# One hand-placed plan for linear attention and a gated unit on one core

## The chip, the core and the metric

The kernel runs on one core of one Trainium2 chip, as one launch. The core has five engines with a queue each: TensorE (PE; its weight loads are shown apart as PEld), VectorE (DVE), ScalarE (ACT), GpSimd (POOL) and SyncE (SP), which only issues transfers here. Each engine takes its instructions in the order in which the program puts them into its queue; semaphores make it wait for the others. Sixteen DMA engines move data between HBM and SBUF. Products land in PSUM, in eight banks.

The metric is the device time of one execution in microseconds (us).

## The reference

Eight batches, eight heads, 576 positions, heads of 64: linear attention without softmax, a norm over each head, and then a gated unit over the 512 columns of all heads.

```python
# q, k, v: (8, 8, 576, 64) float32; w_val, w_out: (512, 512), conv_w: (5, 512), which arrive as float64
kv  = einsum('bhsd,bhse->bhde', k, v)
o   = einsum('bhsd,bhde->bhse', q, kv)
o   = o / sqrt(mean(o*o, -1) + 1e-6) * g_norm
x   = o.transpose(0, 2, 1, 3).reshape(8, 576, 512)
xp  = concat([zeros(8, 4, 512), x], axis=1)
gate_pre = sum(conv_w[t] * xp[:, t:t+576, :] for t in range(5))
gate = 1 / (1 + exp(-gate_pre))
out = (gate * (x @ w_val)) @ w_out
```

## The kernel before

Everything is float32. A batch's positions are taken in 5 chunks of rows (four of 128, one of 64); in a chunk the rows are ordered so that position t*18 + n stands at n*32 + t, which lets the convolution read its five taps as five shifted columns of the same tile (`xT`, with a halo of 4 x 32 columns).

Attention of one batch (`attention(b)`):

- `unit_kv` (line 210), four times, one for each pair of heads: k and v products over 5 pieces of positions into one PSUM tile `kv`; after the fourth VectorE copies it into `kv_bd`, a block-diagonal tile of two heads, and the loads of k and v for batch b + 2 are issued (`load_kv`, line 86; `kl` and `vl` are the last 64 positions, in pieces of 256 bytes).
- `unit_turn_q` (231), four times: VectorE transposes q in blocks of 32 x 32 into `qT`, and the q of batch b + 1 is issued (`load_q`, 103: each row is fetched twice, at two offsets, so that block transposes suffice; 16 transfers of 140 KB for a batch).
- `unit_norm` (238), for each chunk, the short one first: `raw` = q times kv on TensorE (two PSUM banks), squares on ScalarE, sums over a head on VectorE (`ss`), plus epsilon and power -0.5 on GpSimd (`rt`), and the scaled `x` on VectorE.
- `unit_turn_x` (268), two chunks later: TensorE transposes x into PSUM, ScalarE copies it into `xT` with g_norm as scale; after the last chunk but three GpSimd fills the halo.

MLP of one batch (`mlp(b)`):

- `unit_gate` (284), for each of 4 column blocks: ScalarE starts the gate with the last tap, VectorE adds four taps, ScalarE takes the sigmoid.
- `unit_val` (297), for each block: two products of 288 columns (`val`, PSUM tag `mm`, three banks), each multiplied by the gate on VectorE into `gv`.
- `unit_out` (314), 4 or 5 chunks: four products into one bank (tag `mm` as well), a copy on ScalarE into `ot` (three buffers), four stores on SP.

`merge` (353) interleaves the units of attention(b) with those of mlp(b - 1) by their shares of weight, so both lists end together; batch 0's attention is merged with the nine weights (`unit_weights`, 199), which are loaded by GpSimd's queue as 64-bit pairs through three staging buffers and turned into float32 by seven VectorE operations each (`narrow`, 152). The order of the program is not the order in the queues: the framework's scheduler moves instructions by priority and its own estimates of cost.

Most float32 products are two instructions in the trace: the four products of an out chunk are eight rows.

```python
for b in range(B + 1):
    before = mlp(b - 1) if b > 0 else [
        (1.0, lambda n=n: unit_weights(n)) for n in range(len(weights))
    ]
    merge(attention(b) if b < B else [], before)
    if b == 0:
        load_kv(1)
```

Of the kernel before, what the change touches and what calls it, by code (L numbers as in the profile page):

```python
# [9 lines left out]
FP32 = mybir.dt.float32  # L10
# [10 lines left out]
def kernel(  # L21
# [25 lines left out]

    nc = tc.nc
# [15 lines left out]
    S2 = 2 * S  # L64
    assert 2 * T == P and NB * TB == S and SV <= 512 and C <= 512 and D == 2 * TB
# [20 lines left out]
    def load_kv(b):  # L86
        for i in range(2):
            for n, (name, src) in enumerate((("k", k), ("v", v))):
                t = loads.tile([P, H // 2, NJ, D], FP32, tag=f"{name}{i}", name=f"{name}{i}_{b}")
                nc.sync.dma_start(  # L90
                    out=t[:].rearrange("p h j d -> p h (j d)"),
                    in_=src[b, i * H // 2:(i + 1) * H // 2, 0:SF, :].rearrange(
                        "h (p j) d -> p h (j d)", j=NJ),
                )
                st[name, b, i] = t
            if i == 0:
                for n, src in enumerate((k, v)):
# [19 lines left out]
    load_kv(0)  # L117
    for hp in range(HP):
        load_q(0, hp)


    kv_bd = []
    for i in range(2):
        t = const.tile([P, HP, P], FP32, name=f"kvbd{i}")
        nc.vector.memset(t[:], 0.0)
        kv_bd.append(t)
    ident = const.tile([P, P], FP32, name="ident")
    make_identity(nc, ident[:])
    mhalf = const.tile([P, H], FP32, name="mhalf")
    nc.vector.memset(mhalf[:], -0.5)  # L130
    xTs = []
    for i in range(3):
        t = const.tile([P, NK, SX], FP32, name=f"xT{i}")
        for s in range(K - 1):
            nc.gpsimd.memset(t[:, :, s * TB:s * TB + 1], 0.0)
        xTs.append(t)
    gv = const.tile([P, NK, S2], FP32, name="gv")

    gcol = const.tile([P, 1], FP32, name="gcol")
    for r in range(P // D):  # L140
        nc.scalar.dma_start(out=gcol[r * D:(r + 1) * D, :], in_=g_norm.unsqueeze(1))
# [4 lines left out]
    def stage(key, rows):  # L146
        n = rows.shape[0]
        t = loads.tile([P, C, 2], U32, tag="w64", bufs=3, name=f"w64_{key[0]}{key[1]}")
        nc.gpsimd.dma_start(out=t[0:n].rearrange("p c w -> p (c w)"), in_=rows.bitcast(U32))
        staged[key] = t[0:n]  # L150

    def narrow(key, dst):
# [26 lines left out]
        mf = work.tile([P, C], FP32, tag="wmf", name=f"wmf_{key[0]}{key[1]}")[0:n]  # L179
# [4 lines left out]
            out=dst, in0=mf, scalar=2.0 ** -20, in1=e.bitcast(FP32), op0=ALU.mult, op1=ALU.mult,  # L184
        )

    cw = const.tile([K, C], FP32, name="cw")
    wval = const.tile([P, NK, C], FP32, name="wval")
    wout = const.tile([P, NK, C], FP32, name="wout")
    weights = [(("cw", 0), moe_conv_w[:, :], cw[:])]  # L190
    for n, src, dst in (("wval", moe_w_val, wval), ("wout", moe_w_out, wout)):
        for kc in range(NK):
            weights.append(((n, kc), src[kc * P:(kc + 1) * P, :], dst[:, kc, :]))


    nc.vector.tensor_scalar_mul(gcol[:], gcol[:], math.sqrt(D))
    cwT = const.tile([P, NK, K], FP32, name="cwT")

    def unit_weights(n):
        for ahead in range(n + 2 if n else 0, n + 3):  # L200
            if ahead < len(weights):
                stage(*weights[ahead][0:2])
        narrow(weights[n][0], weights[n][2])
        if n == 0:
            cwps = ps("tp", [P, NK, K], "cwps")
            for kc in range(NK):
                nc.tensor.transpose(cwps[:, kc, :], cw[:, kc * P:(kc + 1) * P], ident[0:K, 0:K])
# [196 lines left out]
```

## Time and profile before

| | |
|---|---|
| median of 3 runs | 484.03 us (481.39 to 484.14) |
| the profiled execution | 481.39 us, span 479.6 us |
| mean granted TensorE clock | 0.936 of full speed |
| busy: TensorE, VectorE, ScalarE, GpSimd | 374.6, 235.0, 111.8, 90.0 us |
| moved by DMA | 51.23 MB, mean 107 GB/s |
| the chain that ended last | PE 56%, DVE 17%, POOL 7%, DMA 7%, issue 6%, ACT 4% |

The profile is one execution. The span is the time from the first instruction to the last; the 1.8 us between it and the run's time lie around it. Matmuls are pipelined, so the length of one matmul is longer than the distance to the next one; the price of a product is read from starts. Idle time of an engine that isn't the bottleneck costs nothing.

### The profile page before, as it was taken

The numbers are of one execution on the slowest core, as the hardware profiler recorded it, in microseconds if no ns is written. First come the engines' busy times: TensorE is split into PE (matmuls) and PEld (weight loads), VectorE is DVE, ScalarE is ACT, GpSimd is POOL, SyncE is SP. The second block draws the span as 40 slices with busy tenths as digits, with TensorE's granted clock in tenths as the row PEclk, the third lists the DMA queues.
The fourth block names the chain that finished last, engine by engine and source line by source line (L and its number), as shares of the span: only waits on it lengthen the run. The fifth ranks groups of instructions, "written<-read, shape, count | busy, mean of one in ns | idle before, by whom it ended". The sixth has DMA issues, their size and how long they took to land.

```text
span 479.6 us, 5304 instructions
## 1 busy us (share of the span) xinstructions
PE 374.6 (78%) x1924; PEld 242.0 (50%) x1924; DVE 235.0 (49%) x392; ACT 111.8 (23%) x182; POOL 90.0 (19%) x139
## 2 busy tenths in 40 slices
PE   0412659984798969988897959979797977899895
PEld 0301537464574556655554636645564644565642
DVE  5779459124863385344823356232842348433900
ACT  1000352013412241134101341034111332134201
POOL 2000620026004400071003500062000610341000
PEclk9999979999799988999897898999799798999998
DMA  7997951064004930049502960019800820112012
GB/s 220 280 274 224 276 150 49 0 205 108 1 1 118 273 89 0 1 125 249 125 0 61 246 171 1 0 40 252 196 14 0 225 57 0 45 27 60 1 44 66
DMA packets 39769, 51.23 MB, mean 107 GB/s; under 512 B 13627, under 2 KB 30011, under 8 KB 39744
## 3 DMA queue, kind: packets, MB, share of 16 engines
q1 hardware_dynamic: 38400, 46.68, 37.7%
q0 software_dynamic: 1184, 4.22, 3.1%
q8 instruction: 15, 0.25, 0.2%
q14 instruction: 10, 0.08, 0.1%
q10 hardware_dynamic: 160, 0.00, 0.0%
HBM read 41.44 MB, written 9.44 MB: 106 GB/s over the span
## 4 chain that ended last, share of the span: by engine, by line
PE 56%; DVE 17%; POOL 7%; DMA 7%; issue 6%; ACT 4%; SPq 1%; DVEq 0%; POOLq 0%
PE val L301 22%; PE out L317 21%; DVE gate L290 9%; PE raw L244 8%; POOL rt L258 6%; PE xTps L273 3%; PE kv L218 3%; DMA w_wval<-in_moe_w_val_dram 2%; DVE ss L251 2%; DMA w_wout<-in_moe_w_out_dram 2%; DVE qT L234 2%; DVE x L260 2%; DMA w_cw<-in_moe_conv_w_dram 1%; DMA v<-in_v_dram 1%; ACT gate L287 1%
## 5 line engine op out<-in xcount | busy, mean ns | idle before, releaser
L301 PE MATMUL val<-xT,wval 128*128 128x288 f32 x512 | 145.4, 439 | 12.7 <-DVE gv L307 9.1
L317 PE MATMUL out<-wout,gv 128*128 128x512 f32 x288 | 132.9, 605 | 2.8 <-ACT ot L322 2.4
L301 PEld LDWEIGHTS val<-xT,wval 128*128 128x128 f32 x512 | 101.7, 205 | 44.8 <-DVE gv L307 11.9
L290 DVE SCALAR_TENSOR_TENSOR gate<-xT,cwT,gate 128x576 f32<-128x576 f32 x128 | 97.2, 809 | 35.0 <-ACT gate L287 34.8
L244 PE MATMUL raw<-kvbd,qT 128*128 128x128 f32 (+1 forms) x320 | 62.2, 330 | 60.8 <-DVE qT L234 40.4
L244 PEld LDWEIGHTS raw<-kvbd,qT 128*128 128x128 f32 (+1 forms) x320 | 47.1, 210 | 88.7 <-DVE qT L234 45.2
L317 PEld LDWEIGHTS out<-wout,gv 128*128 128x128 f32 x288 | 53.1, 193 | 56.9 <-issue 52.3
L249 ACT ACTIVATE sq<-raw 128x512 f32<-128x512 f32 (+1 forms) x40 | 23.1, 593 | 191.8 <-PE raw L244 191.7
L258 POOL TENSOR_TENSOR rt<-ss,mhalf 128x8 f32<-128x8 f32 (+1 forms) x40 | 66.7, 1666 | 3.0
L254 POOL TENSOR_SCALAR ss<-ss 128x8 f32<-128x8 f32 (+1 forms) x40 | 9.5, 237 | 305.2 <-DVE ss L251 304.3
L260 DVE TENSOR_TENSOR x<-raw,rt 128x512 f32<-128x512 f32 (+1 forms) x40 | 27.6, 689 | 69.7 <-POOL rt L258 67.6
L307 DVE TENSOR_TENSOR gv<-val,gate 128x288 f32<-128x288 f32 x64 | 28.5, 452 | 51.8 <-PE val L301 50.0
L294 ACT ACTIVATE gate<-gate 128x576 f32<-128x576 f32 x32 | 21.8, 683 | 90.5 <-DVE gate L290 90.2
L251 DVE TENSOR_REDUCE ss<-sq 128x8 f32<-128x512 f32 (+1 forms) x40 | 26.7, 678 | 21.4 <-ACT sq L249 21.3
L276 ACT ACTIVATE xT<-xTps,gcol 128x512 f32<-128x512 f32 (+1 forms) x40 | 25.4, 642 | 39.5 <-PE xTps L273 39.3
L273 PE MATMUL xTps<-ident,x 128*128 128x128 f32 (+1 forms) x160 | 24.8, 285 | 9.6 <-DVE x L260 9.6
L218 PE MATMUL kv<-v,k 128*64 128x64 f32 x512 | 23.8, 236 | 8.9 <-DMA v<-in_v_dram 8.9
L322 ACT COPY ot<-out 128x512 f32<-128x512 f32 x36 | 20.6, 584 | 39.4 <-PE out L317 28.2
L273 PEld LDWEIGHTS xTps<-ident,x 128*128 128x128 f32 (+1 forms) x160 | 19.5, 153 | 18.6 <-issue 18.0
L218 PEld LDWEIGHTS kv<-v,k 128*64 128x64 f32 x512 | 20.5, 148 | 15.8 <-issue 15.6
L234 DVE STREAM_TRANSPOSE qT<-q 128x576 f32<-128x576 f32 x32 | 24.6, 770 | 0.1
L227 DVE COPY kvbd<-kv 64x256 f32<-64x256 f32 x16 | 6.7, 421 | 32.9 <-PE kv L218 32.7
(45 smaller groups left out, 97.2 us busy)
## 6 DMA issues: line engine op xcount, KB each, us to landing
q<-in_q_dram SPq DMA_DIRECT2D x128, 140.0 KB, 3.8
out_dram<-ot SPq DMA_DIRECT2D x144, 64.0 KB, 1.7
k<-in_k_dram SPq DMA_DIRECT2D x16, 512.0 KB, 7.0
v<-in_v_dram SPq DMA_DIRECT2D x16, 512.0 KB, 8.8
w_wval<-in_moe_w_val_dram POOLq DMA_DIRECT2D x4, 512.0 KB, 8.7
w_wout<-in_moe_w_out_dram POOLq DMA_DIRECT2D x4, 512.0 KB, 7.2
kl<-in_k_dram SPq DMA_DIRECT2D x8, 128.0 KB, 8.2
vl<-in_v_dram SPq DMA_DIRECT2D x8, 128.0 KB, 8.1
```

What stands on the lines that cost most here:

```text
L218: nc.tensor.matmul(kvp[r * D:(r + 1) * D, hp, :], st["k", b, half][:, h, j, :] if j < NJ else kl[:, 2 * hp + r, :], st["v", b, half][:, h, ...
L234: nc.vector.transpose(out=st["qT", b][:, hp, :], in_=st["q", b, hp][:, :, 0:TB])
L244: nc.tensor.matmul(raw[0:m, hp * P:(hp + 1) * P], st["qT", b][:, hp, cols], kv_bd[b % 2][:, hp, :], start=True, stop=True,)
L251: nc.vector.reduce_sum(out=ss[0:m], in_=sq[0:m].rearrange("p (h e) -> p h e", h=H), axis=AX.X,)
L258: nc.gpsimd.tensor_tensor(out=rt[0:m], in0=ss[0:m], in1=mhalf[0:m], op=ALU.pow)
L260: nc.vector.tensor_tensor(out=x[0:m].rearrange("p (h e) -> p h e", h=H), in0=raw[0:m].rearrange("p (h e) -> p h e", h=H), in1=rt[0:m].unsq ...
L273: nc.tensor.transpose(px[:, kc, 0:m], st["x", b, c][0:m, kc * P:(kc + 1) * P], ident[0:m, 0:m])
L276: nc.scalar.activation(out=xT[:, :, first:first + m], in_=px[:, :, 0:m], func=AF.Copy, scale=gcol[:],)
L290: nc.vector.scalar_tensor_tensor(out=gate[:], in0=x[:, tap * TB:tap * TB + S], scalar=cwT[:, jt, tap:tap + 1], in1=gate[:], op0=ALU.mult, ...
L301: nc.tensor.matmul(val[:], wval[:, kc, jt * P:(jt + 1) * P], xTs[b % 3][:, kc, HALO + n * SV:HALO + (n + 1) * SV], start=(kc == 0), stop=( ...
L307: nc.vector.tensor_tensor(out=gv[:, jt, first:first + SV], in0=val[:], in1=st["gate", b, jt][:, n * SV:(n + 1) * SV], op=ALU.mult,)
L317: nc.tensor.matmul(po[:], gv[:, jt, c * P:(c + 1) * P], wout[:, jt, :], start=(jt == 0), stop=(jt == NK - 1),)
```

## The change

`merge` and the units of mixed work go. Each step is a function of its own and is put into one list with a time of the author's plan, in units; the list is sorted by that time and issued inside `tc.manual_schedule()`, so that every queue holds its instructions in plan order. What else differs:

- Attention of batch 0 starts at 14, its MLP at 31; attention of batch 1 at 49, 19.8 ahead of its MLP; attention of b >= 2 is put 30 (b = 2) or 34 units ahead of its MLP, its q turns 7 and its kv products 8 units ahead of that, its loads of k and v 25 and of q 22 units ahead.
- q of batches 0 and 1 (`TURNED`) is loaded by rows (`load_q_rows`: 18 transfers of 64 KB, pieces of 256 bytes) and turned by TensorE with a copy on ScalarE (`turn_q_rows`), instead of by VectorE.
- Weights are staged by SP's queue; w_val by blocks of 128 output columns (rows of 1 KB), one narrow covering one val block; conv_w as 20 rows of 128, turned by one transpose instead of four.
- The order of the weight blocks in VectorE's queue is fixed: wval blocks at 17, 20.5, 24 and 27.5, wout blocks at 32, 36, 40 and 44.
- The memsets of the tails move from VectorE to GpSimd, those of the xT edges from GpSimd to VectorE. The gate has five buffers instead of four.

Products, tiles, banks and the arithmetic of each step are as before. The diff, cut to its core:

```diff
+    plan = []
+
+    def at(when, step, *args):
+        plan.append((when, len(plan), step, args))
...
+    def load_q_rows(b, c):
+
+        if c % 2 == 0:
+            st["q2", b] = loads.tile([P, NB, D], FP32, tag="q", bufs=4, name=f"q{b}_{c}")
+        t = st["q2", b][:, c % 2 * H:(c % 2 + 1) * H, :]
+        for j in range(HB if c < NJ else T // TB):
+            nc.sync.dma_start(
+                out=t[j * TB:(j + 1) * TB],
+                in_=q[b].rearrange("h (t n) d -> n t h d", n=NB)[c * HB + j],
+            )
+        st["q", b, c] = t
...
+    def stage(key, src, n, m):
+
+        size = src.shape[-1]
         t = loads.tile([P, C, 2], U32, tag="w64", bufs=3, name=f"w64_{key[0]}{key[1]}")
-        nc.gpsimd.dma_start(out=t[0:n].rearrange("p c w -> p (c w)"), in_=rows.bitcast(U32))
-        staged[key] = t[0:n]
+        t = t[0:n, 0:m * size, :]
+        nc.sync.dma_start(
+            out=t.rearrange("p (m c) w -> p m (c w)", m=m), in_=src.bitcast(U32))
+        staged[key] = t
...
+    def turn_q_rows(b, c):
+        m = size(c)
+        pq = ps("tp", [P, HP, P], f"qTps{b}_{c}")
+        for hp in range(HP):
+            nc.tensor.transpose(
+                pq[:, hp, 0:m], st["q", b, c][0:m, 2 * hp:2 * hp + 2, :], ident[0:m, 0:m])
+        nc.scalar.copy(out=new_qT(b)[:, :, c * P:c * P + m], in_=pq[:, :, 0:m])
...
+    ORDER = [NJ] + list(range(NJ - 1, -1, -1))
+
+    def attention(b, first, step, kv_lead, turn_lead):
+
         for hp in range(HP):
+            at(first - kv_lead + 1.5 * hp, kv_product, b, hp)
+            if b >= TURNED:
+                at(first - turn_lead + 1.5 * hp, turn_q, b, hp)
+        at(first - kv_lead + 1.5 * HP, kv_copy, b)
+        for n, c in enumerate(ORDER):
+            t = first + n * step
+            if b < TURNED:
+                at(t - turn_lead, turn_q_rows, b, c)
+            at(t, raw_product, b, c)
+            at(t + 0.8, square, b, c)
+            at(t + 1.5, scales, b, c)
+            at(t + 4.5, normalise, b, c)
+            at(t + 6.5, turn_x, b, c)
+            at(t + 7.0, keep_x, b, c)
+            if n == 1:
+                at(t + 7.8, halo, b)
+        return first + NJ * step + 7.5
+
+    def gates(b, first, step):
         for jt in range(NK):
+            t = first + step * jt
+            at(t, gate_start, b, jt)
+            for n, tap in enumerate(range(K - 2, -1, -1)):
+                at(t + (n + 1) * step / (K - 1), gate_tap, b, jt, tap)
+            done[b, jt] = t + step + 0.5
+            at(done[b, jt], gate_end, b, jt)
+
+    DV, DO = 2.5, 4.45
+    done = {}
+
+    def mlp(b, first):
+        t = first
+        for jt in range(NK):
+            for n in range(NV):
+                at(t, val_product, b, jt, n)
+                at(max(t + DV, done[b, jt] + 0.1), gated, b, jt, n)
+                t += DV
+        for c in range(NJ) if b % 2 == 0 else range(NJ, 2 * NJ + 1):
+            at(t, out_product, b // 2, c)
+            at(t + DO, store, b // 2, c)
+            t += DO
+
+    begin = [31.0]
+    for b in range(B):
+        begin.append(begin[b] + NK * NV * DV + (NJ + b % 2) * DO)
+    for b in range(B):
         if b == 0:
-            load_kv(1)
+            end = attention(b, 14.0, 2.2, 8.0, 1.0)
+        elif b == 1:
+            end = attention(b, begin[0] + 18.0, 3.0, 8.0, 1.0)
+        else:
+            end = attention(b, begin[b] - min(34.0, 22.0 + 4.0 * b), 3.0, 8.0, 7.0)
+        gates(b, end + 1.0, 3.6 if b < TURNED else 6.5)
+        mlp(b, begin[b])
+
+    at(0.0, stage_weight, "cw", 0)
+    at(0.0, load_kv, 0, 0)
+    at(0.0, set_up)
+    at(0.1, load_kv, 0, 1)
+    for c in ORDER:
+        at(0.2, load_q_rows, 0, c)
+    for jt in range(3):
+        at(0.3, stage_weight, "wval", jt)
+    for i in range(2):
+        at(0.4, load_kv, 1, i)
+    at(5.0, narrow_weight, "cw", 0)
+    at(6.0, turn_cw)
+    when = {}
+    for n in range(2 * NK):
+        key = ("wval", "wout")[n // NK], n % NK
+        when[n] = 17.0 + 3.5 * n if n < NK else 32.0 + 4.0 * (n - NK)
+        at(when[n], narrow_weight, *key)
+        if n >= 3:
+            at(when[n - 3] + 0.1, stage_weight, *key)
+    for n, c in enumerate(ORDER):
+        at(when[1] + 0.2, load_q_rows, 1, c)
+    for b in range(2, B):
+        lead = begin[b] - min(34.0, 22.0 + 4.0 * b)
+        for i in range(2):
+            at(lead - 25.0, load_kv, b, i)
+        for hp in range(HP):
+            at(lead - 22.0 + 0.1 * hp, load_q, b, hp)
+
+    with tc.manual_schedule():
+        for _, _, step, args in sorted(plan, key=lambda p: p[0:2]):
+            step(*args)
```

The steps not shown hold the code of the units they come from: `kv_product` and `kv_copy` (from `unit_kv`), `turn_q`, `raw_product`, `square`, `scales` (the sum on VectorE and the two GpSimd operations) and `normalise` (from `unit_norm`), `turn_x`, `keep_x` and `halo`, `gate_start`, `gate_tap` and `gate_end`, `val_product` and `gated`, `out_product` and `store`.

## Rows read from the trace of the kernel before

**Rows 1.** The page, part 1: busy us, share of the span, instructions.

```profile
PE 374.6 (78%) x1924; PEld 242.0 (50%) x1924; DVE 235.0 (49%) x392; ACT 111.8 (23%) x182; POOL 90.0 (19%) x139
```

**Rows 2.** Four stretches: us, busy PE, PEld, DVE, ACT, POOL, clock, DMA share, GB/s.

```profile
7.50:15.00 7.50, 2.38 (x35) 2.03 (x32) 3.54 (x8) 0.00 (x0) 0.53 (x1) 1.00 1.10 296
12.00:40.00 28.00, 7.30 (x76) 5.72 (x76) 21.54 (x48) 0.00 (x0) 2.65 (x5) 1.00 0.97 264
84.90:143.30 58.40, 47.93 (x330) 32.34 (x329) 26.10 (x42) 13.13 (x21) 10.45 (x14) 0.94 0.23 65
143.30:474.70 331.40, 289.38 (x1389) 180.85 (x1387) 150.17 (x236) 83.92 (x140) 62.93 (x84) 0.93 0.35 89
```

**Rows 3.** The chain that ended last: start us, us, what (x instructions).

```profile
51.95 2.06 PE raw L244 x8
...
75.05 9.97 PE val L301 x40
85.02 8.58 PE out L317 x20
...
143.33 3.43 PE out L317 x8
...
434.90 0.93 PE out L317 x3
435.83 2.59 issue
...
447.51 9.97 PE val L301 x40
```

**Rows 4.** Timeline of TensorE, 188 to 214 us: start us, us, what.

```profile
188.64 2.21 PE L301 MATMUL val<-xT,wval 128*128 128x288 f32 x8
190.78 0.34 PE L218 MATMUL kv<-vl,kl 128*64 128x64 f32 x4
...
191.50 2.21 PE L301 MATMUL val<-xT,wval 128*128 128x288 f32 x8
...
212.61 1.05 PE L244 MATMUL raw<-kvbd,qT 128*128 128x128 f32 x8
213.50 3.60 PE L317 MATMUL out<-wout,gv 128*128 128x512 f32 x8
```

**Rows 5.** The page, part 5: groups, busy us, mean ns, idle before and releaser.

```profile
L290 DVE SCALAR_TENSOR_TENSOR gate<-xT,cwT,gate 128x576 f32<-128x576 f32 x128 | 97.2, 809 | 35.0 <-ACT gate L287 34.8
...
L249 ACT ACTIVATE sq<-raw 128x512 f32<-128x512 f32 (+1 forms) x40 | 23.1, 593 | 191.8 <-PE raw L244 191.7
L258 POOL TENSOR_TENSOR rt<-ss,mhalf 128x8 f32<-128x8 f32 (+1 forms) x40 | 66.7, 1666 | 3.0
...
L260 DVE TENSOR_TENSOR x<-raw,rt 128x512 f32<-128x512 f32 (+1 forms) x40 | 27.6, 689 | 69.7 <-POOL rt L258 67.6
L307 DVE TENSOR_TENSOR gv<-val,gate 128x288 f32<-128x288 f32 x64 | 28.5, 452 | 51.8 <-PE val L301 50.0
L294 ACT ACTIVATE gate<-gate 128x576 f32<-128x576 f32 x32 | 21.8, 683 | 90.5 <-DVE gate L290 90.2
L251 DVE TENSOR_REDUCE ss<-sq 128x8 f32<-128x512 f32 (+1 forms) x40 | 26.7, 678 | 21.4 <-ACT sq L249 21.3
```

**Rows 6.** Line 110, the loads of q: ns on SP min/median/max.

```profile
L110 SPq DMA_DIRECT2D q<-in_q_dram x128: 310/419/2963, 5.0 to 380.9; - x128
```

**Rows 7.** The page, part 3: SP's queue, packets, MB, share of 16 engines.

```profile
q1 hardware_dynamic: 38400, 46.68, 37.7%
```

**Rows 8.** Timeline of VectorE, 9.5 to 11.8 us, narrow of conv_w.

```profile
9.89 0.41 DVE L168 TENSOR_SCALAR wexp_cw<-wexp_cw 5x512 uint32<-5x512 uint32 x1
10.34 0.68 DVE L171 SCALAR_TENSOR_TENSOR wexp_cw<-w_cw,wexp_cw 5x512 uint32<-5x512 uint32 x1
11.05 0.68 DVE L183 SCALAR_TENSOR_TENSOR cw<-wmf_cw,wexp_cw 5x512 f32<-5x512 f32 x1
```

**Rows 9.** Timeline, 464 to 480 us: the last copy on ScalarE.

```profile
474.72 0.58 ACT L322 COPY ot<-out 128x512 f32<-128x512 f32 x1 [2.85 <-DMA out_dram<-ot]
```

More of the change, by code (lines that the diff above doesn't have):

```diff
@@ new lines, with set_up @@
+    cw = const.tile([NK * K, P], FP32, name="cw")
+    cwT = const.tile([P, K, NK], FP32, name="cwT")
+    wval = const.tile([P, NK, C], FP32, name="wval")
+    wout = const.tile([P, NK, C], FP32, name="wout")
+    def set_up():
+        make_identity(nc, ident[:])
+        for pair in tails:
+            for t in pair:
+                nc.gpsimd.memset(t[T:P], 0.0)
+        for t in kv_bd:
+            nc.vector.memset(t[:], 0.0)
+        nc.vector.memset(mhalf[:], -0.5)
+        for t in xTs:
+            for s in range(K - 1):
+                nc.vector.memset(t[:, :, s * TB:s * TB + 1], 0.0)
+        for r in range(P // D):
+            nc.scalar.dma_start(out=gcol[r * D:(r + 1) * D, :], in_=g_norm.unsqueeze(1))
@@ L297, in unit_val @@
[L297 to L310 removed]
+            out=xTs[b % 3][:, :, first:first + m], in_=st["px", b, c][:, :, 0:m],
@@ new lines, in gate_tap, with gate_end, val_product @@
+    def gate_tap(b, jt, tap):
+        gate = st["gate", b, jt]
+        nc.vector.scalar_tensor_tensor(
+            out=gate[:], in0=xTs[b % 3][:, jt, tap * TB:tap * TB + S],
+            scalar=cwT[:, tap, jt:jt + 1], in1=gate[:], op0=ALU.mult, op1=ALU.add,
+        )
+    def gate_end(b, jt):
+        gate = st["gate", b, jt]
+        nc.scalar.activation(out=gate[:], in_=gate[:], func=AF.Sigmoid)
+    def val_product(b, jt, n):
+        val = ps("mm", [P, SV], f"val{b}_{jt}_{n}")
+        for kc in range(NK):
+            nc.tensor.matmul(
+                val[:], wval[:, kc, jt * P:(jt + 1) * P],
+                xTs[b % 3][:, kc, HALO + n * SV:HALO + (n + 1) * SV],
+                start=(kc == 0), stop=(kc == NK - 1),
+            )
+        st["val", b, jt, n] = val
@@ L312, with gated, out_product @@
+    def gated(b, jt, n):
+        first = b % 2 * S + n * SV
+        nc.vector.tensor_tensor(
+            out=gv[:, jt, first:first + SV], in0=st["val", b, jt, n][:],
+            in1=st["gate", b, jt][:, n * SV:(n + 1) * SV], op=ALU.mult,
+        )
     rows_out = out.rearrange("b (t n) c -> b n t c", n=NB)
-    def unit_out(i, c):
+    def out_product(i, c):
         po = ps("mm", [P, C], f"out{i}_{c}")
```

249 lines of the change are left out of this document (90 added, 159 removed).

## The prediction, made blind

> **What bounds the kernel now.** I read the page's busy times first, then the chain that ended last, then three stretches, and last the prices of single instructions.
>
> TensorE is the busiest engine and VectorE is at half [rows 1]. A share over the span hides three stages, so look at the stretches [rows 2]. From 12 to 40 us the DMA moves 264 GB/s at a share of 0.97 while TensorE works 7.3 of 28 us: loading and VectorE set the pace. From 84.9 to 143.3 TensorE is busy 47.9 of 58.4 us. From 143.3 to the last matmul at 474.7 it is busy 289.4 of 331.4 us at a granted clock of 0.93, that is, part of the time at 1.2 instead of 2.4 GHz. So 42 us of that stretch are idle, and some of the busy time is half-speed.
>
> The chain says where the idle time sits [rows 3]. Batch 0's val products run dense from 75.05 and its first out product starts at 85.0; batch 1's out products start at 143.3. The last batch boundary is the pattern: `out` stops at 436, and dense `val` starts at 447.5. There are seven such boundaries, one before each of batches 1 to 7; this one costs 11.7 us. The reason is in the order: the attention of batch b finishes only when the MLP of b-1 finishes, and then x, its transpose and the five-tap gate must go through before `val` can be consumed.
>
> **Dense prices.** By the distance from one start to the next [rows 4]: a val product (8 instructions) 2.14 us, the four-step share of kv for one pair of heads 0.72 (190.78 to 191.50), a raw product of 128 rows 0.89. An out product is 3.43 [rows 3]. A transpose of x is taken as half a raw product, 0.45, since it has half the instructions. The raw product of 64 rows isn't there alone; I take 1.4, between 0.9 and the slow 2.06 [rows 3]. A batch is then 8 x 2.14 + 4.5 x 3.43 + (4 x 0.89 + 1.4) + 5 x 0.45 + 4 x 0.72 = 17.1 + 15.4 + 5.0 + 2.2 + 2.9 = 42.6 us, and 8 batches 341 us: that is what TensorE has to do at full clock.
>
> **The change, stage by stage.**
>
> *Order.* The plan puts attention b 30 to 34 units ahead of mlp(b) from batch 2 on, and its units come out as about 1 us of TensorE: one batch is 20 + 17.8 or 22.25 units, mean 40, against my 42.6. Gates of batch b >= 3 begin 13.5 units ahead of their first val product. So the boundary wait goes, if no engine falls behind. VectorE per batch: 16 taps x 0.81, 5 x (0.68 + 0.69) for scales and normalise, 8 x 0.45 for gated [rows 5], 4 q turns at about the price of a tap, 0.8 for kv_copy: 27.5 of 42.6 us. GpSimd has 5 x (1.67 + 0.24), about 10, ScalarE 5 x (0.6 + 0.65) + 4 x (0.75 + 0.68) + 4.5 x 0.6, about 15 (0.24, 0.65, 0.75 and 0.6 for the unlisted ones are estimates beside the listed [rows 5]). None is near the bound. What VectorE now waits for in its own queue: normalise(c) stands three units behind scales(c) and must see GpSimd's 1.67 us; the taps put between cover it. Raw has two banks, so raw(c) needs normalise(c-2), planned 1.5 units earlier; in the attention window three units hold some 4 us of TensorE work, and the chain raw, square, reduce, pow, multiply is 0.89 + 0.6 + 0.68 + 1.9 + 0.69 = 4.8 plus handovers. I cost all this at 0.7 us a batch, 4 us.
>
> *Start of the first batch.* Weights leave GpSimd's queue for SP's, behind all of kv(0) and q(0). Ahead of the first wval block are 2.36 + 1.18 + 0.52 MB (itself in); at 264 GB/s [rows 2] that is 15.4 us, from about 2.5 us on, and about 2 to land: 20 us. SP's 18 issues for q, 0.42 each as now [rows 6], end at about 13 and don't bind. q(0) now comes as 4,608 pieces of 256 bytes. Price of a piece unknown: from below its bytes, 4.5 us for q(0); from above the mean of all packets, 37.7% x 479.6 x 16 / 38,400 = 75 ns each [rows 7], 21.6 us, which would put wval at 36. I take the lower end: 7.5 to 15 us, when 256-byte tail rows of k and v came in, moved 296 GB/s, no less than elsewhere [rows 2].
> The Trainium skill (DMA: Bandwidth & Descriptors, Specifications) says that transfers under 512 B go below line rate, by read-modify-write; counted as 512 B each, q(0) would cost 4.5 us more and the time would be some 4 us higher, an estimate. The trace leans against it by the 296 GB/s above.
>
> VectorE runs in plan order, and scales(0,4) is done at about 16, so it stands at narrow(wval 0) until 20. One narrow is seven operations, most of them dependent on the one before: 0.45 apart, 0.71 for the long ones [rows 8], 3.75 us in all (before, its steps were interleaved). Up to normalise(0,0): three narrows 11.3, 4 scales 2.7, 5 normalise 3.5, waits where scales stands right behind the normalise that frees its raw bank (raw 0.9 to 2, square 0.6), 2 x 2.2, and one for pow, 1.5: 43.4. One transpose and copy later, at 44.8, val may start. That alone gains nothing, since each val product must be taken out of its bank by gated, and VectorE still has: narrow wval 3 (47.1), four wout narrows 15.0, 16 taps 13.3 (0.83 with the gap), 7 gated 3.2, two sigmoid waits 1.7, kv_copy(1) 0.8: 81.1. Then scales(1,4) waits for raw and square (1.7) and takes 0.7, and gated(0,3,1) 0.45: out(0,0) starts at **84**, where it was 85.0 [rows 3]. All of VectorE's list is the path here; the q turn on TensorE takes 2 x 4 x 0.8 = 6.2 us off it and adds 10 x 0.45 to TensorE and 10 copies of about 0.7 to ScalarE, hidden in batch 0 since both idle there. The rest of the set-up costs nothing: the memsets that change engine and the smaller narrow and single transpose of the conv weights end before 16 us, covered by the wait for wval; without that cover the conv part would cost some 3 us. Each later weight block waits on SP for a staging buffer, that is for the narrow three before it, with q(1) and then kv(2) and q(2) behind it; kv(1) and q(1), 3.5 MB, are not wanted before 77.
>
> *Batch 1.* On SP, q(2) waits for the tiles of q(1), until about 99, and holds the stores of batch 0 behind it; three output buffers cover that. Batch 1's attention begins at out(0,0). TensorE's queue alternates out, turn_q_rows, raw; raw must wait for ScalarE's copy of q each time (0.85), as nothing stands between. Out 4 x 3.43, raw 4 x 0.89, turns 9 x 0.45, copies 4 x 0.85 = 24.7, and the last chunk's way through normalise, turn and keep adds what isn't covered: 26. val(1) starts at **110**. VectorE then sets the pace once more: 16 taps 13.3, turn_q(2) 3.1, kv_copy 0.8, 8 gated 3.6, 3 scales and 2 normalise 3.4, waits for sigmoid and pow 2.5: 26.7. out(0,4) starts at **137**, 6 us before 143.3.
>
> *The rest.* TensorE's list from there: out(1) 5 x 3.43 = 17.2; val of six batches 102.7; their 27 out products 92.6; attention of five batches 5 x 10.1 = 50.5; what is left of attention 2, 2 raw and 5 turns, 4.0: 267. It ends at 404. The same list, with some 6 us more of attention 2, took 331.4 [rows 2]: that is where 58 us go, 42 of idle time and the rest half-clock and slower raw products.
> Then 4 us for small waits, and 5.0 from the last matmul to the end as now (the last copy starts at 474.72 [rows 9], span 479.6): span 413. The profiled run's time is 1.8 above its span, 415; the median of the runs shown lies 0.5% above that run, 2 us: **416 us**, 0.86 of 484.03.
>
> **Rivals.**
> 1. *VectorE becomes the bound.* In-order waits behind pow and sigmoid are exposed. For it: 27.5 of 42.6 us, and before, VectorE lost 67 us waiting for pow by its own row, x after rt [rows 5]. Against: two units to three with taps between. If three chunks a batch show 1.5 us each, six batches cost 27 us less the 4 counted: 439.
> 2. *The start is worse.* The 256-byte rows cost the upper end, 16 us: 432. Less of it is likelier.
> 3. *The start is better.* No raw-bank waits, narrows at 3.4 us: 12 us less, 404 or, without small waits, 400.
> 4. *Slower than before, by late loads.* SP's queue holds loads and stores in one order; k, v and q of a batch are 4.6 MB, 17.4 us at 264 GB/s, issued 25 units ahead of attention, so that q has some 5 us of slack. A store that waits for ScalarE holds back the loads behind it. From 11 us late per batch over six batches it is no gain; at half the rate (17.4 us more, 12 past the slack, plus a clock fall) it is 72 us: 488. Against: the DMA share is 0.35 in that stretch [rows 2].
> 5. *The order changes nothing*, since the boundary is refilled by other waits of the same size: within 1% of 484.
>
> **Chances.** Forecast (402 to 428) 0.66; rival 1, 0.14; rival 2, 0.07; rival 3, 0.08; rivals 4 and 5, 0.03 and 0.02. Range for 8 in 10: 400 to 437, which takes in most of 1, 2 and 3; all but rivals 4 and 5 have the same sign. A measurement can tell about 1% from no change. Faster 0.95, same 0.02, slower 0.03.
>
> **What would show it.** Right: out(0,0) within 5 us of 84; first val near 45; after 140 no stretch over 2 us in which TensorE waits for a tap or gated; granted clock above 0.97 there; per batch 42 to 44 us. Wrong: wval landing far from 20 us; raw waiting for normalise by several us a batch (rival 1); kv or turn_q waiting for DMA (rival 4); or a dense TensorE that takes more than 43 us a batch, which would make my prices too low.

## The result, and the profile after

The kernel after takes 406.0 us (median of 4 runs, 404.6 to 407.7) where the kernel before takes 482.7 (481.0 to 484.1) on the same chip: a ratio of 0.841, with a 95% interval of 0.836 to 0.847. The profiled run took 407.7 us, its span is 405.9. The forecast was 416, its range 400 to 437.

The page of the kernel after, part 1 and some groups of part 5 (columns as in [rows 1] and [rows 5]):

```profile
PE 358.3 (88%) x1961; PEld 238.9 (59%) x1961; DVE 231.8 (57%) x392; ACT 117.7 (29%) x192; POOL 98.7 (24%) x122
...
L289 POOL TENSOR_SCALAR ss<-ss 128x8 f32<-128x8 f32 (+1 forms) x40 | 16.9, 423 | 253.6 <-DVE ss L286 253.6
L293 POOL TENSOR_TENSOR rt<-ss,mhalf 128x8 f32<-128x8 f32 (+1 forms) x40 | 70.0, 1750 | 3.3
...
L299 DVE TENSOR_TENSOR x<-raw,rt 128x512 f32<-128x512 f32 (+1 forms) x40 | 27.6, 689 | 56.6 <-POOL rt L293 56.6
```

TensorE is busy 88% of the span, from 78% [rows 1]. VectorE still waits 57 us behind pow, from 68 [rows 5]; these waits didn't go, but from out(0,4) on they hardly reach TensorE.

The stages of the kernel after, cut at the first val product, out(0,0), val(1) and out(0,4) (columns as in [rows 2]):

```profile
0.00:50.00 50.00, 23.84 (x161) 20.11 (x161) 23.72 (x62) 10.06 (x16) 15.04 (x24) 0.89 0.83 205
50.00:86.30 36.30, 26.40 (x157) 19.16 (x157) 32.17 (x57) 7.08 (x11) 0.00 (x0) 0.83 0.09 29
86.30:114.70 28.40, 24.87 (x102) 14.08 (x101) 7.14 (x11) 9.65 (x18) 10.48 (x14) 0.93 0.56 146
114.70:140.70 26.00, 24.26 (x173) 18.47 (x173) 20.59 (x32) 7.15 (x12) 4.05 (x4) 0.93 0.89 239
140.70:401.30 260.60, 258.92 (x1373) 167.08 (x1372) 148.18 (x232) 83.16 (x137) 69.18 (x81) 1.00 0.41 104
```

The last row answers to the last of [rows 2]. The stretch from out(0,4) to the end of the last matmul took 331.4 us and takes 260.6: 70.8 of the span's 73.7 us. TensorE's idle time in it falls from 42.0 to 1.7 us, its busy time from 289.4 to 258.9, and the granted clock rises from 0.93 to 1.00, the upper of the two levels (2.4 GHz). The start gives 2.6 more, with out(0,4) at 140.7 instead of 143.3, and the tail 0.3. From val(1) to val(7), six batches, it was 316.8 us and is 253.7, that is 52.8 and **42.3 us a batch**. The same kernel in another execution (e9, below) has first val at 49.7, out(0,0) at 85.8, val(1) at 113.8 and out(0,4) at 138.7, so the stage times of two profiles can differ by 2 us without any change.

What TensorE waits for, by line and releaser (us in total, times, longest), before, from val(1) at 122.8 to val(7) at 439.6:

```profile
PE raw L244 <- DVE qT L234: 20.6, 6, 5.2
PE raw L244 <- DVE x L260: 9.0, 9, 2.1
PE val L301 <- DVE gv L307: 7.2, 5, 3.7
```

and after, from 141 to 401 us, the whole list:

```profile
PE raw L271 <- DVE x L299: 1.6, 3, 0.7
```

A boundary after, on TensorE's timeline (start us, us, what): the out products behind batch 4's val products and the first val of batch 5, with nothing between:

```profile
274.70 10.46 PE L367 MATMUL out<-wout,gv 128*128 128x512 f32 x24
285.00 2.10 PE L348 MATMUL val<-xT,wval 128*128 128x288 f32 x8
```

And the last boundary before, for which the prediction read 11.7 us out of [rows 3]:

```profile
434.74 3.60 PE L317 MATMUL out<-wout,gv 128*128 128x512 f32 x8
...
439.64 6.09 PE L301 MATMUL val<-xT,wval 128*128 128x288 f32 x24 [0.87 <-ACT xT L276]
447.51 2.69 PE L301 MATMUL val<-xT,wval 128*128 128x288 f32 x10 [1.78 <-DVE gv L307]
```

The chain shows only what the end hung on. TensorE itself worked in between, on out until 438.3 and on three val products from 439.6, and was idle for 2.65 us.

The start came later than forecast. Its VectorE timeline (in brackets the wait before, and for what):

```profile
19.28 0.68 DVE L286 TENSOR_REDUCE ss<-sq 64x8 f32<-64x512 f32 x1 [2.80 <-ACT sq L280]
23.57 0.43 DVE L178 TENSOR_SCALAR wexp_wval<-w_wval 128x512 uint32<-128x512 uint32 x1 [3.61 <-DMA w_wval<-in_moe_w_val_dram]
...
31.61 0.69 DVE L286 TENSOR_REDUCE ss<-sq 128x8 f32<-128x512 f32 x1 [2.86 <-ACT sq L280]
...
39.53 0.69 DVE L286 TENSOR_REDUCE ss<-sq 128x8 f32<-128x512 f32 x1 [2.86 <-ACT sq L280]
```

and SP's queue (start us, us held, what it issued):

```profile
6.09 12.30 SPq L149 DMA_DIRECT2D q<-in_q_dram  x18
18.43 1.55 SPq L163 DMA_DIRECT2D w_wval<-in_moe_w_val_dram  x3
```

SP needs 12.3 us for the 18 issues of q(0), so wval isn't issued before 18.43 and VectorE stands until 23.57. The issues are not evenly spaced: the first nine take 7.9 us, the last nine 0.49 each, like the 18 of q(1) (8.8 us from 35.77). What holds the first ones is in the trace: wherever it has the landing of the transfer eight places ahead in SP's order (284 of SP's 333 issues), the issue starts after that landing, and 42 start within 0.1 us of it; the issues wait on eight semaphores in turn. The seventh and the eighth of q(0) start at 11.07 and 13.14, each 0.02 us behind the landing of the last k and the last v of batch 0. SP's own waits from 5 to 19 us, after and then the longest of before's:

```profile
SPq L149 <- DMA v<-in_v_dram: 1.7, 1, 1.7
SPq L149 <- DMA k<-in_k_dram: 0.4, 1, 0.4
```

```profile
SPq L110 <- DMA v<-in_v_dram: 2.7, 1, 2.7
```

Then two scales wait 2.86 us each for raw and square of a chunk whose bank the normalise just ahead of them had freed.

### The profile page after: what moved, and what is told of

It is laid out like the page before. It is cut to its first block, busy times and chain, and to the rows that moved or that the text cites. A ratio compares the mean times of both kernels' runs of the same rounds, so it can differ in the third digit from the quotient of the medians.

```text
span 405.9 us, 5359 instructions
## 1 busy us (share of the span) xinstructions
PE 358.3 (88%) x1961; PEld 238.9 (59%) x1961; DVE 231.8 (57%) x392; ACT 117.7 (29%) x192; POOL 98.7 (24%) x122
## 4 chain that ended last, share of the span: by engine, by line
PE 62%; DVE 16%; DMA 8%; SPq 5%; ACT 3%; POOL 3%; issue 3%; DVEq 0%; ACTq 0%
PE out L367 25%; PE val L348 22%; PE raw L271 8%; DVE gate L336 5%; PE xTps L311 3%; PE kv L236 3%; DMA v<-in_v_dram 3%; DMA q<-in_q_dram 2%; POOL rt L293 2%; SPq L378 2%; DMA out_dram<-ot 2%; DMA w_wval<-in_moe_w_val_dram 1%; SPq L118 1%; DVE x L299 1%; SPq L149 1%
## 5 line engine op out<-in xcount | busy, mean ns | idle before, releaser
L348 PE MATMUL val<-xT,wval 128*128 128x288 f32 x512 | 141.1, 425 | 6.3 <-DVE gv L357 4.7
L367 PE MATMUL out<-wout,gv 128*128 128x512 f32 x288 | 129.3, 601 | 0.0
L348 PEld LDWEIGHTS val<-xT,wval 128*128 128x128 f32 x512 | 96.8, 196 | 35.0 <-DVE gv L357 5.6
L336 DVE SCALAR_TENSOR_TENSOR gate<-xT,cwT,gate 128x576 f32<-128x576 f32 x128 | 102.9, 810 | 21.2 <-ACT gate L330 19.3
L289 POOL TENSOR_SCALAR ss<-ss 128x8 f32<-128x8 f32 (+1 forms) x40 | 16.9, 423 | 253.6 <-DVE ss L286 253.6
L293 POOL TENSOR_TENSOR rt<-ss,mhalf 128x8 f32<-128x8 f32 (+1 forms) x40 | 70.0, 1750 | 3.3
L271 PE MATMUL raw<-kvbd,qT 128*128 128x128 f32 (+1 forms) x320 | 48.8, 301 | 22.7 <-DVE x L299 12.0
L271 PEld LDWEIGHTS raw<-kvbd,qT 128*128 128x128 f32 (+1 forms) x320 | 43.7, 198 | 32.9 <-issue 17.2
L330 ACT ACTIVATE gate<-xT,cwT 128x576 f32<-128x576 f32 x32 | 24.5, 771 | 0.2
L254 DVE STREAM_TRANSPOSE qT<-q 128x576 f32<-128x576 f32 x24 | 18.3, 768 | 0.0
```

The source lines that it names most:

```text
L271: nc.tensor.matmul(raw[0:m, hp * P:(hp + 1) * P], st["qT", b][:, hp, c * P:c * P + m], kv_bd[b % 2][:, hp, :], start=True, stop=True,)
L293: nc.gpsimd.tensor_tensor(out=rt[0:m], in0=ss[0:m], in1=mhalf[0:m], op=ALU.pow)
L330: nc.scalar.activation(out=gate[:], in_=xTs[b % 3][:, jt, HALO:SX], func=AF.Copy, scale=cwT[:, K - 1, jt:jt + 1])
L336: nc.vector.scalar_tensor_tensor(out=gate[:], in0=xTs[b % 3][:, jt, tap * TB:tap * TB + S], scalar=cwT[:, tap, jt:jt + 1], in1=gate[:], op ...
L348: nc.tensor.matmul(val[:], wval[:, kc, jt * P:(jt + 1) * P], xTs[b % 3][:, kc, HALO + n * SV:HALO + (n + 1) * SV], start=(kc == 0), stop=( ...
L367: nc.tensor.matmul(po[:], gv[:, jt, c * P:(c + 1) * P], wout[:, jt, :], start=(jt == 0), stop=(jt == NK - 1),)
```

## The experiments

All are edits of the kernel after. Each ratio is to the kernel before on the same chip; what is called better or more is so against 406.0 us, unless another base is named.

### What the lead is worth: e1_short_lead, e2_mid_lead, e10_mid_lead

```diff
-            end = attention(b, begin[b] - min(34.0, 22.0 + 4.0 * b), 3.0, 8.0, 7.0)
-        gates(b, end + 1.0, 3.6 if b < TURNED else 6.5)
+            end = attention(b, begin[b] - 20.5, 3.0, 8.0, 7.0)
+        gates(b, end + 1.0, 3.6)
```

(the loads' `lead` follows; e2 has 27.0 and the old gates, e10 has 27.0 and gates of step 6.2)

> Attention of batches 2 to 7 is put 20.5 units ahead of its MLP instead of 30 or 34, so it ends when the MLP before it ends and the gates start with the first val product, as in the kernel before; everything stays placed by hand. Theory (the lead is what removes the wait at the batch boundary): six boundaries cost again about 8 us each, the chain of the last chunk that isn't covered plus VectorE's 5.1 us for a gate against 4.3 us for its two val products; 406 + 48 = about 450 us (430 to 465), TensorE waits for xT, gated and taps in each boundary and the granted clock falls after some. Rival (a fixed hand order by itself, without the lead, brings the gain): within 10 us of 406.

> The lead of attention for batches 2 to 7 is 27 units instead of 30 or 34, the gates' step is kept. Theory (the lead only has to cover the chain of the last chunk and the first gate): nearly all of the gain stays, 406 to 414 us, since the first gate is still done before the third val product needs its bank. Rival (each unit of lead counts): half-way to the run with 20.5 units, some 425 us.

> The lead of attention for batches 2 to 7 is 27 units instead of 30 or 34, and the gates' step is 6.2 instead of 6.5 units, so that the last gate block stands before the first out product in the plan. Theory now (each batch loses what its chain lacks in lead, as gates and the next attention then press on VectorE at the same time): 43.5 to 44.5 us a batch between 42.3 (lead 34) and 46.0 (lead 20.5), 414 to 418 us. Rival (the lead is worth nothing past the first gate): 406 to 409.

e1: 431.6 us, ratio 0.897 (0.8945 to 0.8996). e2: 416.9, 0.867 (0.865 to 0.870); in it the first out product of batches 2 to 7 reads the last gate block's part of gv before it is multiplied, so it is no clean measure of the lead. e10: 409.8, 0.850 (0.847 to 0.853), against 406.8 for the kernel after on the same chip (e9).

So the lead, with the gates' step that goes with it, pays 25 us between 20.5 units and 34, and only 3 between 27 and 34: it saturates. Both expectations on it, 450 for e1 and 414 to 418 for e10, were too high. In e1, from val(1) to val(7) (stretch as in [rows 2]) and TensorE's waits there:

```profile
113.30:389.40 276.10, 257.45 (x1440) 169.15 (x1440) 155.10 (x240) 80.55 (x136) 62.86 (x84) 0.98 0.48 128
```

```profile
PE raw L271 <- DVE kvbd L246: 11.6, 3, 4.0
PE val L348 <- ACT xT L318: 4.7, 6, 0.8
PE val L348 <- DVE gv L357: 1.7, 3, 0.7
```

Without the lead, TensorE is idle for 18.7 us (276.1 less 257.45), where after has 3.4 and before 42, at clock 0.98: 46.0 us a batch. The first wait is that of attention for VectorE's kv_copy. In the plan kv_copy stands two units ahead of the first raw in every version, but with the short lead the taps of the batch before and the turns of q fill VectorE's queue right ahead of it (at the first of the three places VectorE has no gap from 171.2 to 180.1, and kv_copy starts at 178.7); the other two are the old boundary, val behind x's transpose and behind gated, at under 1 us each. The order placed by hand shortens the boundary by itself; the lead removes what is left.

### The same plan, left to the framework's scheduler: e3_auto

```diff
-    with tc.manual_schedule():
-        for _, _, step, args in sorted(plan, key=lambda p: p[0:2]):
-            step(*args)
+    for _, _, step, args in sorted(plan, key=lambda p: p[0:2]):
+        step(*args)
```

> The same steps in the same plan order, but outside the block of manual_schedule, so the framework's scheduler may move instructions between them by its own costs. Theory (what counts is attention ahead of the MLP, which the program order still asks for): 400 to 425 us. Rival (the scheduler undoes the plan, as its estimates of cost pull attention and MLP together again): above 440 us, with waits at the batch boundaries.

469.5 us, ratio 0.978 (0.975 to 0.980). The rival holds: a plan whose order isn't kept is worth 2%. From val(1) to val(7), and the largest waits of TensorE there:

```profile
104.50:430.10 325.60, 275.75 (x1406) 172.33 (x1404) 158.33 (x249) 85.30 (x141) 63.05 (x84) 0.95 0.38 100
```

```profile
PE raw L271 <- DVE x L299: 16.4, 9, 3.8
PE xTps L311 <- DVE x L299: 16.1, 12, 1.9
PE val L348 <- DVE gv L357: 11.7, 18, 1.4
```

54.3 us a batch, where before had 52.8: 50 us idle, behind x and gated again. Its gain is all from the start, and there it beats the plan kept by hand: val(1) at 104.5 and out(0,4) at 123.7, against 114.7 and 140.7. So the plan's start can be bettered.

### How near VectorE is to being the bound: e4_more_dve

```diff
+        if b >= TURNED:
+            spare = work.tile([P, S], FP32, tag="spare", bufs=1, name=f"spare{b}_{jt}")
+            nc.vector.scalar_tensor_tensor(
+                out=spare[:], in0=xTs[b % 3][:, jt, 0:S], scalar=cwT[:, 0, jt:jt + 1],
+                in1=xTs[b % 3][:, jt, HALO:SX], op0=ALU.mult, op1=ALU.add,
+            )
```

One tap more behind each gate block of batches 2 to 7: 24 x 0.81 = 19.4 us of VectorE's time.

> One more VectorE operation of the size of a tap (0.81 us) behind each gate of batches 2 to 7, on data that nothing reads: 24 operations, 19.4 us of VectorE. Theory (from 141 us on TensorE sets the pace and VectorE has slack): at most 4 us more, 406 to 410. Rival (VectorE is the bound there, or as good as): about 19 us more, 425.

411.5 us, ratio 0.855 (0.854 to 0.857): 5.5 more than after, a little over the 4 that were expected at most. From out(0,4) to the end of the last matmul, and TensorE's wait for x there:

```profile
138.70:405.00 266.30, 260.04 (x1374) 167.10 (x1372) 165.41 (x256) 83.22 (x137) 74.53 (x81) 1.00 0.40 101
```

```profile
PE raw L271 <- DVE x L299: 5.8, 7, 1.6
```

VectorE isn't the bound, or 19 us would show, but the cover isn't whole: over a quarter of the added work comes through, and the wait for x that shows was 1.6 us and is 5.8. TensorE sets the pace with little room.

### What the start waits for: e5_two_queues, e6_pool_weights, e7_narrow_between

```diff
-            nc.sync.dma_start(
+            (nc.scalar if b == 0 and j % 2 else nc.sync).dma_start(
```

> Every second row transfer of q for batch 0 is issued by ScalarE's queue instead of SP's; bytes, pieces and their order within a queue stay. In the changed kernel SP needs 12.3 us for its 18 issues, and the first wval block is issued at 18.4 and read at 23.6, while the DMA share is 0.63 to 0.73 from 15 to 20 us. Theory (SP's issuing holds the weights back, not the bytes): wval is issued some 5 us earlier and lands by about 20, VectorE's wait of 3.6 us before its first narrow goes, and as VectorE sets the pace up to 141 us the whole is 3 us shorter, 403. Rival (256-byte pieces keep the DMA engines busy until 20 us): wval is issued earlier but lands at 23 to 24 all the same, no change, 406.

404.4 us, ratio 0.838 (0.836 to 0.840): 1.7 better, which is within the spread of the kernel after's own runs (404.6 to 407.7). In the profile the first narrow begins at 21.17, 2.4 earlier, and out(0,4) at 136.7. SP's nine issues still take 8.66 us, though one by itself takes only 0.31 to 0.46: they too wait for the transfer eight places ahead. The DMA shows the rest (stretches as in [rows 2]; the share adds up the time of all packets, so it can pass 1), after and then e5:

```profile
12.50:15.00 2.50, 1.83 (x34) 1.83 (x36) 0.00 (x0) 0.00 (x0) 0.00 (x0) 1.00 1.20 164
15.00:17.50 2.50, 2.04 (x20) 1.73 (x17) 0.84 (x2) 0.37 (x1) 0.00 (x0) 1.00 0.63 134
```

```profile
12.50:15.00 2.50, 1.30 (x24) 1.33 (x26) 0.00 (x0) 0.00 (x0) 0.00 (x0) 1.00 1.25 175
15.00:17.50 2.50, 1.99 (x27) 1.69 (x25) 0.84 (x2) 1.66 (x2) 0.00 (x0) 1.00 0.78 163
```

At 12.5 to 15 the DMA engines are full in both (1.20 and 1.25) and yet move 164 and 175 GB/s: all 1,697 packets of after there, and 1,764 of e5's 1,777, are under 512 bytes. From 15 on they are not full (0.63, then 0.78). In after SP issues 64 KB every 0.49 us then, which makes 133 GB/s, an estimate, and 134 are moved: the issues set the pace. Landings, rows and issues each hold up a part; what each is worth in the whole time wasn't separated.

```diff
-        nc.sync.dma_start(
+        nc.gpsimd.dma_start(
```

(in `stage_weight`)

> All weights are staged by GpSimd's queue, as in the kernel before, instead of SP's. Theory (the weights stand behind 24 issues on SP and come too late by 3.6 us): the first wval block lands before 17 us, VectorE's wait for it goes; but half of kv(0) shares the DMA with 1.5 MB of weights and lands 2 to 3 us later, which takes part of it back: 402 to 406. Rival (the weights' place in the queues is worth more, as VectorE can narrow while it waits for attention): under 400. Second rival (k and v land so late that the start is worse): above 408.

405.7 us, 0.840 (0.838 to 0.842): no change. The narrow no longer waits for wval, but scales(0,4), ahead of it in VectorE's order, now comes at 21.82 instead of 19.28, so that the narrow begins at 22.42 instead of 23.57. The wait has moved to the chunk's square, and little is won.

```diff
-        when[n] = 17.0 + 3.5 * n if n < NK else 32.0 + 4.0 * (n - NK)
+        when[n] = (17.0, 18.6, 20.8, 23.0)[n] if n < NK else 32.0 + 4.0 * (n - NK)
```

> In VectorE's queue three of the wval narrows move by some units (18.6, 20.8, 23 instead of 20.5, 24, 27.5), so that each stands between a normalise and the scales behind it. Theory (VectorE is the path of the start, and it waits there three times, 2.9 us each, for raw and square of a chunk whose bank the normalise in front has just freed): two or three of these waits are filled with narrows; out(0,0) starts 6 us earlier and the whole takes 400 us. Rival (TensorE or the loads set the start): no change, 406, as the waits move elsewhere.

400.3 us, 0.829 (0.827 to 0.831): 5.7 better, as much as the two waits of 2.86. A narrow now stands between each normalise and the next scales, and the two reduces on VectorE's timeline have no bracket:

```profile
31.19 0.68 DVE L286 TENSOR_REDUCE ss<-sq 128x8 f32<-128x512 f32 x1
...
36.16 0.68 DVE L286 TENSOR_REDUCE ss<-sq 128x8 f32<-128x512 f32 x1
```

out(0,0) comes at 79.1 and out(0,4) at 133.2, some 7 us earlier than in the profile of after, 6.7 and 5.5 earlier than in e9's. Up to out(0,0) VectorE's list is the path, as the prediction had it.

### q of batches 0 and 1 by VectorE again: e8_turned0

```diff
-    TURNED = 2
+    TURNED = 0
```

(with `load_q` in place of `load_q_rows` for both batches, and the plan's times for a turn by VectorE)

> q of batches 0 and 1 is loaded twice-offset and turned by VectorE like that of the other batches (16 transfers of 140 KB a batch, 4 turns of 0.77 us), the rest of the plan stays. Theory (the turn on TensorE saves VectorE, which sets the pace of the start, 6.2 us, half of it while VectorE waits for data anyway, and 1.1 MB less is loaded ahead of the weights): 3 to 8 us more, 409 to 414. Rival (256-byte pieces and ScalarE's copies cost as much as they save): 404 to 408.

405.3 us, 0.840 (0.838 to 0.843): no difference from after, so the theory of 3 to 8 us more fell. What the turn on TensorE gains in batch 0 it gives back in batch 1: without it out(0,0) comes at 90.4, 4 to 5 later, but val(1) at 113.5 and out(0,4) at 138.4, no later than in e9 (113.8 and 138.7). TensorE's timeline of batch 1's attention, after and then e8:

```profile
94.11 0.60 PE L263 MATMUL qTps<-ident,q 128*128 128x128 f32 x4
95.44 1.16 PE L271 MATMUL raw<-kvbd,qT 128*128 128x128 f32 x8 [0.73 <-ACT qT L265]
96.43 3.60 PE L367 MATMUL out<-wout,gv 128*128 128x512 f32 x8
```

```profile
96.16 1.95 PE L271 MATMUL raw<-kvbd,qT 128*128 128x128 f32 x16
97.94 3.60 PE L367 MATMUL out<-wout,gv 128*128 128x512 f32 x8
```

After, each raw stands 0.67 to 0.73 us behind ScalarE's copy of q, and the nine turns (0.6 us each as listed, overlapping what follows) come on top. e8's loads of q(0), 16 x 140 KB = 2.24 MB instead of 1.18, hold SP for 10.96 us instead of 12.30, and the last of them lands at 20.6 where the last of after's lands at 20.2: half the bytes in 256-byte rows are hardly faster. The stretch in which after moves 164 GB/s is in e8:

```profile
12.50:15.00 2.50, 1.97 (x37) 1.98 (x38) 0.18 (x1) 0.00 (x0) 0.00 (x0) 1.00 1.03 317
```

### Attention of batch 1 earlier: e11_attn1_early

```diff
-            end = attention(b, begin[0] + 18.0, 3.0, 8.0, 1.0)
+            end = attention(b, begin[0] + 7.0, 3.0, 8.0, 1.0)
```

> Attention of batch 1 (and its gates behind it) is put 11 units earlier in the plan, at 38 instead of 49, so that it stands among the val products of batch 0. Theory (in the changed kernel VectorE is full from 50 to 86 us while TensorE is busy 26 of 36 us, and nearly idle, 7 of 28 us, from 86 to 115, where TensorE does out(0) and attention 1 in turn and waits; then gates(1) hold up val(1) until 141): out(0,0) starts up to 7 us later, at 90 to 93, but gates(1) run beside the out products of batch 0 and out(0,4) starts at 126 to 132 instead of 140.7; 393 to 399 us. Rival (VectorE's list up to out(0,4) is the path whatever its order): 404 to 408, as the 84 us of VectorE's work end at the same time.

397.4 us, 0.8235 (0.820 to 0.827): 9.4 better than after on the same chip (e9). The rival, that VectorE's list up to out(0,4) is the path whatever its order, fell. Two stretches:

```profile
50.00:86.00 36.00, 27.80 (x180) 20.98 (x178) 33.49 (x59) 10.80 (x17) 5.70 (x4) 0.82 0.09 30
86.00:120.00 34.00, 33.23 (x196) 21.30 (x196) 21.64 (x32) 12.32 (x20) 7.16 (x10) 1.00 0.57 150
```

out(0,0) is later, at 92.1 for 86.3, as VectorE has more to do ahead of it; but some of batch 1's attention is then done, the stretch after it is dense (33.2 of 34 us, clock 1.00), and val(1) comes at 106.7 for 114.7 (113.8 in e9).

### The kernel after again, and all three together: e9_after_again, e12_all

e9 is the kernel after, unchanged; e12 has the edits of e5, e7 and e11.

> The changed kernel once more, unchanged, beside the three runs of this set, so that differences under 1% are read on one chip. Both theories: 404 to 408 us.

> Three edits together: attention of batch 1 11 units earlier, wval narrows between normalise and scales, every second row transfer of q(0) issued by ScalarE's queue. Theory (all three act on the start, before TensorE sets the pace, one behind the other): the gains add, 10 + 6 + 2 us less than the changed kernel, 386 to 392 us. Rival (they remove the same waits twice): no better than the best of them alone, 396 to 400.

e9: 406.8 us, 0.843 (0.840 to 0.846). e12: 390.2, 0.809 (0.806 to 0.8125), 16.6 under e9; the parts alone give 1.7, 5.7 and 9.4 less than the kernel after, 16.8. So they add, to within the 1 or 2 us by which runs differ, and e12 beats both kernels. Its two late stretches:

```profile
82.00:105.00 23.00, 22.53 (x95) 13.25 (x96) 13.80 (x20) 9.72 (x16) 4.76 (x8) 1.00 0.64 165
121.00:383.00 262.00, 259.78 (x1381) 167.77 (x1380) 148.15 (x232) 83.91 (x138) 70.00 (x81) 1.00 0.45 115
```

From 121.85 us on it is the kernel after: the same 260 us of TensorE's work, begun 19 us earlier than in the profile of after and 17 earlier than in e9's.

## Why the prediction was right, point by point

The forecast's span is 413: out(0,4) at 137, 267 of dense work, 4 of small waits, 5 of tail. Measured: 140.7, 260.6 with the waits in it, 4.6, together 405.9. So the start was 3.7 us worse and the rest 10.8 better than forecast, and the total is nearer than its parts because these two run against each other. The last term, 2 us by which the median would lie above the profiled run, came out as 1.7 below it.

- **The boundary.** Right in what goes, wrong in what it consisted of. The 58 us expected of the stretch after 143 are 71: no wait of TensorE over 0.7 us, clock 1.00, 42.3 us a batch against a forecast of 42.6. But the 11.7 us of one boundary were read from the chain, and seven of them would be 82 where only 42 were idle; TensorE's timeline has 2.65 us idle there. About half of the idle time was not behind x, its transpose or the gate: the largest wait, 20.6 us in six places, was raw's for q turned by VectorE, whose turns stood among the taps in VectorE's queue (the longest, 5.2 us until 398.4, for a turn that followed eight taps, from 391.7 to 397.6). It went with the others. The sum didn't need this split, since it took all idle time away. That the placed order does it is shown by e3, which has the same plan without it. The lead alone does less than the prediction's wording says: e1 keeps two thirds of the gain without it (431.6 of 482, where after is 406.0).
- **The clock.** Taking all busy time at full clock was right. From val(1) to val(7), nearly the same products, before, e3, e1 and after are idle for 42.0, 49.9, 18.7 and 3.4 us, at granted clocks of 0.93, 0.95, 0.98 and 0.99 and with 274.9, 275.8, 257.5 and 250.3 us busy. The clock goes with the idle time in these four; no run changes one without the other.
- **Dense prices.** Slightly high: 258.9 us busy for 267. A val product takes 2.04 us (285.00 to 287.04), not 2.14: 48 of them make 4.8 us. The raw product of 64 rows, for which 1.4 was taken between 0.9 and 2.06, takes 1.02 (252.55 to 253.57): 5 make 1.9. A kv share takes some 0.65 (287.04 to 288.35 for two), not 0.72: 20 make 1.3. Together 8.0 of the 8.1 us; the rest, smaller, cancels. An out product, 10.30 / 3 = 3.43, was right.
- **Small waits.** 0.7 us a batch was allowed, 4 in all; 1.7 came. Rival 1 fell, but e4 shows how near it was: with 19.4 us more on VectorE over six batches the waits for x begin to reach TensorE.
- **SP's issues "end at about 13 and don't bind".** Wrong, and the step that cost most at the start. The price was nearly right: the median issue takes 0.45 us for the 0.42 of [rows 6], and 0.49 from one start to the next. What the sum left out is that an issue waits for the landing of the transfer eight places ahead; behind the 2.4 MB of k and v the first nine take 7.9 us, and all end at 18.39. Before has such waits too (2.7 us for v, above). wval is issued 5 us later than forecast and read at 23.57, not 20.
- **256-byte rows.** "I take the lower end" was wrong. The row that it went by, 296 GB/s with tail rows of k and v, had few of them: 656 of 1,912 packets, and 0.17 of 2.22 MB, were that short. With q(0) alone in the queue, the engines are full at a share of 1.20 and move 164 GB/s; e8 moves 317 GB/s in the same 2.5 us at a share of 1.03. By that rate the 1.18 MB take 7.2 us where 264 GB/s give 4.5, an estimate of 2.7 us more; what the whole time sees of it wasn't measured by itself.
  The Trainium skill (DMA: Bandwidth & Descriptors, Specifications), that transfers under 512 B fall below line rate, agrees with these rows; the trace of before didn't "lean against it", as hardly any of its bytes came in such transfers.
- **First val.** 50.1 against 44.8: 3.6 from wval, 1.3 from two bank waits of 2.86 instead of 2.2, and 0.4 from small differences. That the waits are on the path was right: e7 takes them out and wins 5.7.
- **out(0,0).** 86.3 against 84, since VectorE's list from first val on took 36.2 us, 3.0 less than the 39.2 forecast. That this list is the path holds (32.2 of 36.3 us busy).
- **val(1).** 28.4 us after out(0,0), forecast 26. The first out product took 5.58 us (86.26 to 91.84) instead of 3.43: the granted clock was 0.63 in it, that is, most of the time at the lower level (1.2 GHz), after 6.3 us in which TensorE was busy for 1.9. The waits for ScalarE's copy, four at 0.67 to 0.73, were sized right (0.85).
- **"The q turn on TensorE takes 6.2 us off" VectorE's path.** The work is taken off (VectorE 237.0 us busy in e8, 231.8 after), but the time isn't: e8 is as fast. The sum looked at batch 0, where the engines that take over do idle, and priced the same turn in batch 1, where TensorE is the path, without setting the two against each other. (2 x 4 x 0.8 is 6.4; the 6.2 fits the 0.77 of a turn.)
- **Late loads** (rival 4) didn't come: no wait of TensorE for a load of k, v or q after 141 us.

## What to carry to other kernels

Where the trace shows TensorE's order, and not its work, making the idle time, cost the dense list; in this kernel nearly all the rest came back, but only with the placed order kept to the chip: the same plan given back to a scheduler was worth 2% instead of 16%. Read the idle time from TensorE's own waits, not from the chain. A lead pays up to a point: 27 units gave all but 3 us of what 34 give, while a start planned step by step (other work between a freed bank and its next reader, the next attention begun before the path needs it) brought another 4%. The cost of an issue is its own time plus its wait: here no transfer was seen to be issued on SP before the one eight places ahead had landed, so what stands behind large loads goes out late, however cheap an issue is.

## What was not expected of the hardware

GpSimd's small add, one instruction with the same operands in both kernels, takes 0.42 us in the mean where it took 0.24, and its pow 1.75 where it took 1.67 [rows 5]. The add's group before:

```profile
L254 POOL TENSOR_SCALAR ss<-ss 128x8 f32<-128x8 f32 (+1 forms) x40 | 9.5, 237 | 305.2 <-DVE ss L251 304.3
```

One by one, after: 27 of the 40 adds take 0.23 to 0.34 us, and the 13 that run beside a tap of VectorE (two inputs in SBUF) 0.74 to 1.10. A pair of chunks on GpSimd's timeline of the kernel after, and then VectorE's at the same time:

```profile
214.97 1.10 POOL L289 TENSOR_SCALAR ss<-ss 64x8 f32<-64x8 f32 x1 [25.50 <-DVE ss L286]
216.16 2.19 POOL L293 TENSOR_TENSOR rt<-ss,mhalf 64x8 f32<-64x8 f32 x1
219.75 0.24 POOL L289 TENSOR_SCALAR ss<-ss 128x8 f32<-128x8 f32 x1 [1.40 <-DVE ss L286]
220.07 1.67 POOL L293 TENSOR_TENSOR rt<-ss,mhalf 128x8 f32<-128x8 f32 x1
```

```profile
215.18 1.65 DVE L336 SCALAR_TENSOR_TENSOR gate<-xT,cwT,gate 128x576 f32<-128x576 f32 x2
```

The slow pair lies over two taps. The quick one starts beside a gated product (219.59 to 220.03, one of its inputs in PSUM), and then VectorE waits for it. Before, no add ran beside a tap, as attention and gates took turns. The Trainium skill (Advanced Engine Details and Errata, GPSIMD Details) says that GpSimd shares a read and a write interface with VectorE and conflicts with its instructions that have two SBUF inputs; these rows agree, and the longest add is 0.87 us over the shortest, about one tap (0.81). Other runs bear out that it is the taps. In e1 no add runs beside one, and all 40 take 0.23 to 0.34 us. In e10 five do, at 0.74 each. In e4, which adds nothing but operations of the tap's kind, 15 do, at 0.74 to 2.56, and the other 25 take 0.23 to 0.34. After 141 us TensorE waits no more than 1.6 us in all for x, which needs the pow behind these adds, so here it costs next to nothing, but it is a price of overlapping the two.
